# Decode attention on one core: V's fifth tile loaded ahead of K's fifth, DVE's small steps moved behind K's turns, q's copies on ACT, w2 in five pieces

## The chip, the core and the metric

The kernel runs on one core of a Trainium2 chip. The core has five engines that run side by side, each through its own list of instructions in order: TensorE (PE; PEld is its weight load), VectorE (DVE), ScalarE (ACT), GpSimd (POOL) and SyncE (SP), which here issues nearly all DMAs. An instruction waits at the head of its engine's list until the semaphores that it needs are set, and what stands behind it waits too. The metric is the device time of one execution in microseconds (us).

## The reference

One decode step of a transformer block, for 8 sequences with one new token each, all in float32. A conditioning vector c gives six modulations; attention runs over a window of the K and V caches; a feed-forward part with a squared ReLU follows.

```
mod = silu(c) @ w_mod                      # 8 x (6*512): sa, ca, ga, sb, cb, gb
h = layernorm(x) * (1 + ca) + sa           # x: 8 x 1 x 512
q = h @ wq                                 # 32 query heads of 128, 8 key/value heads
k, v = the last 2048 of 8192 cached rows   # 8 sequences x 8 heads x 2048 x 128 each
p = softmax(q k^T / sqrt(128));  o = p v
x = x + ga * (o @ wo)                      # wo: 4096 x 512
h = layernorm(x) * (1 + cb) + sb
x = x + gb * (relu(h @ w1 + b1)^2 @ w2 + b2)   # w1: 512 x 1792, w2: 1792 x 512
```

The K and V windows are 67 MB each, the weights some 31 MB: 165 MB are read for little arithmetic.

## The kernel before, in words

**Tiles and slots.** All loads from HBM go into two sets of buffers in on-chip memory: 2 big slots of 4 MB (`K_SLOTS`) and 5 small ones of 2 MB (`V_SLOTS`). A K tile (`("K", q)`, q = 0 to 15) is half of the sequences of one key/value head and takes a big slot; a V tile (`("V", n)`, n = 0 to 31) is two sequences of one head and takes a small one. w_mod (three pieces) and wo (three tiles of two heads each; the fourth lies in the tail) take small slots, wq (two halves), the tail (last part of wo, first half of w1) and w2 take big ones. With two big slots, K tile q can be loaded only when K tile q - 2 has been used up.

**The order of the loads** is a list, `loads` (L144 to L155), written ahead of time. `pump` (L158) issues its entries in order as long as the next one has a free slot; `done` (L163) frees a slot and pumps. All loads stand in SP's one list, so a load that waits for its slot holds all loads behind it. w2 is issued in four pieces (L136), so that its matmuls can start on the first.

**The main loop** (L494) has 38 steps of a quarter of a head. A step s turns half a K tile: `transposes` (L195) is DVE's 32x32 block transpose of 128x1024 elements, called a turn below, four turns a step; two make one kT tile, of which there are two buffers. `scores` (L349) multiplies it with q on TensorE, four column groups into one PSUM bank `s_ps` for a head. The big slot is free after a tile's eighth turn (L196).

**Softmax of a head** is spread over the two steps behind its last scores. ACT copies the scores out of PSUM (`ss`, L370); DVE takes the maximum of each row (`mx`, L372); TensorE permutes the scores (`p_ps`, L377) and turns the maxima into a row (L380); DVE reduces them over four rows and scales them (`m`, `mrow`, L383, L389); TensorE turns them back into a column; DVE copies it (`nm`, L398); ACT takes the exponential with the row sums `z` (L401) and half of the spread-out copy `pr2` (L409), DVE the other half (L411) and `zs` (L413); DVE transposes it (`pT`, L423), TensorE sums over rows (L428), DVE takes the reciprocal `rz` (L432).

**P V** runs five steps behind (`PV_LAG`). `weighted` (L434) multiplies pT with a V tile in two halves on TensorE; after the second half the V slot is free, and four DVE instructions (L457, L459) add the diagonal blocks into `o_sb`. `gather` (L463) and `project_o` (L478) bring a head's output through wo.

**q.** Two `turn_q` calls (L319) turn the query into `qbd`, the second one at step 1. `window` (L337) spreads one head's q over the four column groups into `qst`: one matmul and eight copies of 32x64 out of PSUM, by turns on ACT and DVE (L345). The first head's stands in front of the first scores, each next head's in front of the scores in the middle of the head before.

**The end.** When the last V tile has been used, the output projection, the second layer norm, w1 and w2 follow, each on the one before; w2's matmuls (L606) go through its 14 row blocks in order.

Of the kernel before, what the change touches and what calls it, by code (L numbers as in the profile page):

```python
# [20 lines left out]
def tile_adaln_cached_attention_mlp(  # L21
# [26 lines left out]
    C = B // 2  # L48
    N = HKV * C
# [39 lines left out]
    def load(key):  # L89
        kind, i = key  # L90
        if kind == "b":
            nc.sync.dma_start(b1_in, b1.rearrange("(g n) -> g n", g=NQ))
            nc.sync.dma_start(b2_in, b2.rearrange("(g n) -> g n", g=NQ))
            return
        held[key] = free[size_of(key)].pop(0)
        t = slots[size_of(key)][held[key]]
        if kind in "KV":


            if kind == "K":  # L100
                v = k_cache[4 * (i % 2) : 4 * (i % 2) + 4, i // 2]
            else:
                v = v_cache[i % C :: C, i // C]
            v = v[:, SK - W :, :].rearrange("u (p j) d -> p u (j d)", p=P // v.shape[0])
            for x in range(2 if key == ("V", N * 2 - 1) else 1):
                cols = slice(x * NJ * DH // 2, (x + 1) * NJ * DH // 2) if key == ("V", N * 2 - 1) else slice(None)
                nc.sync.dma_start(t[:, cols], v[..., cols])
            return

        def rows(o, v):  # L110
            n = v.shape[1] * v.shape[2]
            nc.sync.dma_start(t[:, o : o + n].rearrange("p (a n) -> p a n", n=v.shape[2]), v)

        def wo_rows(j):

            r = 2 * REP * DH
            return wo[j * r : (j + 1) * r, :].rearrange("(h p i) n -> p h (i n)", p=P, i=4)

        w1v = w1.rearrange(r_kc, p=P)
        if kind == "wo":  # L120
            rows(0, wo_rows(i))
        elif kind == "mod":

            nc.sync.dma_start(t, w_mod.rearrange("(p kc) n -> p (kc n)", p=P)[:, i * NJ * DH : (i + 1) * NJ * DH])
        elif kind == "wq":

            nc.sync.dma_start(t, wq.rearrange("(p h a) n -> h p (a n)", p=P, h=2)[i])
        elif kind == "tail":
            for h in range(2):
                rows(h * 4 * D, wo_rows(HKV // 2 - 1)[:, h : h + 1])  # L130
            rows(NJ * DH, w1v[:, 0:2])
        elif kind == "w1":
            rows(0, w1v[:, 2:4])
        else:
            v = w2.rearrange("(p c) n -> p c n", p=P)
            for lo, hi in ((0, 8), (8, 12), (12, 13), (13, 14)):  # L136
                rows(D * lo, v[:, lo:hi])

    def slot(key, n, o=0):
# [2 lines left out]
        return t[:, : t.shape[1] // n * n].rearrange("p (a n) -> p a n", n=n)  # L142

    loads = [*(("mod", k) for k in range(3)), ("wq", 0), ("wq", 1)]  # L144
    loads += [("V", 0), ("K", 0), ("V", 1), ("K", 1), ("V", 2), ("K", 2), ("V", 3), ("K", 3), ("K", 4)]
    late = N // 4
    for v in range(4, N):

        q, odd = divmod(v + 4 if v <= 2 * late - 4 else v + 5, 2)
        if not odd and 4 < q < N // 2:  # L150
            loads.append(("K", q))
        if v % (2 * C) == 2 * C - 4 and v < 6 * C:
            loads.append(("wo", v // (2 * C)))
        loads.append(("V", v))
    loads += [("b", 0), ("tail", 0), ("w1", 0), ("w2", 0)]  # L155
# [25 lines left out]


    qbd = consts.tile([P, HKV, 4, B * REP], F32, name="qbd")
    qst = [consts.tile([P, B, 4, 4, 2, REP], F32, name=f"qst{i}") for i in range(2)]


    KTS = {}
# [142 lines left out]
            )  # L330

    turn_q(0)


    PT_, RZ_, RZP_, OS_, O_, MX_, SS_, X_ = {}, {}, {}, {}, {}, {}, {}, {}

    def window(hk):  # L337

        pq = ps_1.tile([P, 512], F32, name="q_ps")
        nc.tensor.matmul(pq[:, :P], sel, qbd[:, hk].rearrange("p j x -> p (j x)"), start=True, stop=True)  # L340
        pv = pq[:, :P].rearrange("p (j c u t) -> p c u j t", j=4, c=2, u=4)
        for i in range(4):
            b = slice(32 * i, 32 * i + 32)
            for c in range(2):
                (nc.vector.tensor_copy if c else nc.scalar.copy)(  # L345
                    qst[hk % 2][b, 4 * c : 4 * c + 4, :, i, c], pv[b, c]
                )

    def scores(q, j):  # L349

        hk, c = divmod(q, 2)
        if c == 0 and j == 0:
            s_ps[0] = ps_1.tile([P, 512], F32, name="s_ps")
            if hk == 0:
                window(0)
        if c == 1 and j == 0 and hk + 1 < HKV:
            window(hk + 1)
        kT = KTS.pop((q, j)).rearrange("q r (p u) -> q u (r p)", u=4)
        for u in range(4):
            nc.tensor.matmul(  # L360
                s_ps[0][32 * u : 32 * u + 32, :],
                qst[hk % 2][:, 4 * c + u, j].rearrange("p i c t -> p (i c t)"),
                kT[:, u],
                start=(c == 0 and j == 0),
                stop=(c == 1 and j == 3),
            )

    def soft_a(hk):
        ss = work.tile([P, 512], F32, name="ss", tag="a", bufs=1)
        nc.scalar.copy(ss, s_ps[0])  # L370
        mx = work.tile([P, 1], F32, name="mx")
        nc.vector.tensor_reduce(mx, ss, axis=AX.X, op=ALU.max)  # L372
        SS_[hk], MX_[hk] = ss, mx

    def soft_b(hk):
        sp = ps_1.tile([P, 512], F32, name="p_ps")
        nc.tensor.matmul(sp, perm, SS_.pop(hk), start=True, stop=True)  # L377
        SS_[hk] = sp
        pm = ps_m.tile([P, 512], F32, name="m_ps", tag="m_ps")
        nc.tensor.matmul(pm[0:1, :P], MX_.pop(hk), ident, start=True, stop=True)  # L380
        mrow = work.tile([1, 4, 32], F32, name="mrow")
        m1 = work.tile([1, 32], F32, name="m1")
        nc.vector.tensor_reduce(  # L383
            m1.rearrange("p (u r) -> p u r", u=4),
            pm[0:1, :P].rearrange("p (u i r) -> p u r i", u=4, i=4),
            axis=AX.X,
            op=ALU.max,
        )
        nc.vector.tensor_scalar(mrow, m1[:, None, :].to_broadcast([1, 4, 32]), -SCALE, None, op0=ALU.mult)  # L389
        MX_[hk] = mrow  # L390

    def soft_c(hk):
        pm = ps_m.tile([P, 512], F32, name="m_ps", tag="m_ps")
        nc.tensor.matmul(
            pm[:, 0:1], MX_.pop(hk).rearrange("p j r -> p (j r)"), ones[0:1, 0:1], start=True, stop=True
        )
        nm = work.tile([P, 1], F32, name="nm")
        nc.vector.tensor_copy(nm, pm[:, 0:1])  # L398
        pr = work.tile([P, 2, 32, 8], F32, name="pr", tag="a", bufs=1)
        z = work.tile([P, 1], F32, name="z")  # L400
        nc.scalar.activation(  # L401
            pr.rearrange("p e j x -> p (e j x)"), SS_.pop(hk), AF.Exp, bias=nm, scale=SCALE, accum_out=z
        )

        X_[hk] = work.tile([P, 32, 8, 2, 2], F32, name="pr2", bufs=1)
        for c in range(2):
            o, i = X_[hk][:, :, :, :, c], pr.rearrange("p e j x -> p j x e")
            if c:
                nc.scalar.mul(o, i, uq[:, c : c + 1])  # L409
            else:  # L410
                nc.vector.tensor_scalar(o, i, uq[:, c : c + 1], None, op0=ALU.mult)  # L411
        zs = work.tile([P, B], F32, name="zs")
        nc.vector.tensor_scalar(zs, bq, z, None, op0=ALU.mult)  # L413
        RZP_[hk] = zs
# [19 lines left out]
    def weighted(n, h):  # L434
# [6 lines left out]
        for g in range(4):  # L441
# [8 lines left out]
        if h == 0:  # L450
            return
        del O_[n]
        done(("V", n))
# [24 lines left out]
    def project_o(hk):  # L478
# [11 lines left out]
        if hk % 2 and not last:  # L490
            done(("wo", hk // 2))


    for s in range(N + PV_LAG + 1):  # L494
        g, i = divmod(s, C)
# [157 lines left out]
```

## Time and profile before

| | |
|---|---|
| median of 3 runs | 402.33 us (402.02 to 403.03) |
| the profiled execution, its own time | 402.6 us |
| its span, from the first to the last instruction | 400.7 us |
| TensorE busy, DVE busy, ACT busy | 261.9, 246.2, 33.5 us |
| moved by DMA, mean over the span | 165.08 MB, 412 GB/s |
| chain that ended last: DMA, DVE, PE | 63%, 21%, 11% |

How to read it: the page cuts the span into 40 slices, each digit being a busy share in tenths. In the rows of groups and of the timeline stand line, engine, operation, what is written <- what is read, the shape, and in brackets how long the engine idled before it and what ended that. SPq rows are DMA issues; their time is the issue's, not the transfer's. In the chain of waits a DMA row starts at the issue and ends at the landing, so it holds the time that the transfer queued behind others.

### The profile page before, as it was taken

How to read it: one execution, taken by the hardware profiler on the slowest of the kernel's cores; microseconds unless marked ns; L12 is line 12 of the kernel's file. 1: busy time of each engine (PE TensorE's matmuls, PEld its weight loads, DVE VectorE, ACT ScalarE, POOL GpSimd, SP SyncE). 2: the span in 40 equal slices, each digit the busy share in tenths (PEclk: the TensorE clock that was granted, in tenths of full speed). 3: DMA queues.
4: the chain of work that ended last, by engine and by line, in shares of the span. 5: the costliest groups of instructions: out<-in, count | busy, mean ns of one | idle time of the engine just before them, and what ended most of it. 6: DMA issues, size and time to landing. Idle time of an engine off the chain costs nothing.

```text
span 400.7 us, 3775 instructions
## 1 busy us (share of the span) xinstructions
PE 261.9 (65%) x1502; PEld 58.7 (15%) x1502; DVE 246.2 (61%) x436; ACT 33.5 (8%) x81; POOL 0.9 (0%) x7
## 2 busy tenths in 40 slices
PE   0624517656777865887488738974855678867595
PEld 0301101001111110211021102110211011111133
DVE  1630157847867775787578847975738478954331
ACT  1200010002001000100010001000100010030010
POOL 0000000000000000000000000000000000000000
PEclk9978857886989989898999978988997989999799
DMA  8999999995899999999999999999999999999993
GB/s 316 447 432 415 444 429 415 451 422 224 366 406 433 429 442 417 436 425 435 411 448 412 450 409 442 419 440 411 443 415 451 406 443 415 432 430 421 421 426 151
DMA packets 9922, 165.08 MB, mean 412 GB/s; under 512 B 1064, under 2 KB 1328, under 8 KB 1584
## 3 DMA queue, kind: packets, MB, share of 16 engines
q1 hardware_dynamic: 9760, 164.71, 96.6%
q8 instruction: 12, 0.20, 0.2%
q10 hardware_dynamic: 144, 0.13, 0.2%
q14 instruction: 6, 0.05, 0.0%
HBM read 164.77 MB, written 0.07 MB: 411 GB/s over the span
## 4 chain that ended last, share of the span: by engine, by line
DMA 63%; DVE 21%; PE 11%; ACT 2%; issue 1%; SPq 0%; DVEq 0%; ACTq 0%
DMA big<-in_A_k_cache_dram 39%; DVE kT L195 14%; DMA small<-in_A_v_cache_dram 12%; DMA big<-in_A_wq_dram 7%; DMA big<-in_B_w_dram 6%; PE s_ps L360 5%; DVE o_sb L459 3%; PE o_ps L443 3%; DVE qst L345 1%; PE m_ps L309 1%; ACT qst L345 1%; DVE o_sb L457 1%; PE p_ps L377 0%; PE m_ps L606 0%; ACT L401 0%
## 5 line engine op out<-in xcount | busy, mean ns | idle before, releaser
L360 PE MATMUL s_ps<-kT,qst 128*32 128x512 f32 x512 | 127.4, 1074 | 93.5 <-DVE kT L195 77.1
L195 DVE STREAM_TRANSPOSE kT<-big 128x1024 f32<-128x1024 f32 x128 | 151.7, 1219 | 48.4 <-DMA big<-in_A_k_cache_dram 48.3
L443 PE MATMUL o_ps<-small,pT 128*32 128x512 f32 x512 | 74.3, 653 | 7.8 <-DMA small<-in_A_v_cache_dram 7.7
L459 DVE SCALAR_TENSOR_TENSOR o_sb<-o_ps,diag,o_sb 128x128 f32<-128x128 f32 x96 | 33.7, 351 | 3.4
L360 PEld LDWEIGHTS s_ps<-kT,qst 128*32 128x32 f32 x512 | 12.1, 119 | 140.5 <-DVE kT L195 82.3
L443 PEld LDWEIGHTS o_ps<-small,pT 128*32 128x32 f32 x512 | 17.4, 121 | 77.4 <-issue 56.1
L457 DVE TENSOR_SCALAR o_sb<-o_ps,diag 128x128 f32<-128x128 f32 x32 | 10.4, 326 | 19.1 <-PE o_ps L443 19.1
L309 PE MATMUL m_ps<-big,h1T 128*32 128x512 f32 x64 | 10.0, 784 | 12.4 <-DMA big<-in_A_wq_dram 12.4
L327 DVE COPY qbd<-m_ps 32x128 f32<-32x128 f32 x8 | 3.0, 372 | 23.1 <-PE m_ps L324 23.0
L345 ACT COPY qst<-q_ps 32x64 f32<-32x64 f32 x32 | 6.5, 204 | 117.8 <-PE q_ps L340 78.7
L370 ACT COPY ss<-s_ps 128x512 f32<-128x512 f32 x8 | 4.7, 586 | 98.8 <-PE s_ps L360 98.8
L377 PE MATMUL p_ps<-ss,perm 128*128 128x512 f32 x16 | 11.6, 813 | 0.0
L345 DVE COPY qst<-q_ps 32x64 f32<-32x64 f32 x32 | 6.8, 213 | 6.6 <-ACT qst L345 6.5
L401 ACT ACTIVATE pr<-p_ps,nm 128x512 f32<-128x512 f32 x8 | 5.5, 688 | 62.5 <-DVE nm L398 62.5
L467 PE MATMUL m_ps<-o_sb,pick 128*128 128x512 f32 x16 | 9.0, 644 | 2.6 <-DVE o_sb L459 2.6
L423 DVE STREAM_TRANSPOSE pT<-pr 128x1024 f32<-128x1024 f32 x8 | 9.8, 1229 | 0.0
L411 DVE TENSOR_SCALAR pr<-pr,uq 128x512 f32<-128x512 f32 x8 | 4.0, 500 | 8.5 <-ACT pr L401 8.5
L383 DVE TENSOR_REDUCE m<-m_ps 1x32 f32<-1x128 f32 x8 | 2.2, 277 | 11.0 <-PE m_ps L380 11.0
L229 PE MATMUL m_ps<-xsum,sel 128*128 128x1 f32 x2 | 0.6, 363 | 12.7 <-DVE xsum L227 12.7
L372 DVE TENSOR_REDUCE mx<-ss 128x1 f32<-128x512 f32 x8 | 5.2, 654 | 4.4 <-ACT ss L370 4.4
L283 PE MATMUL m_ps<-small,cT 128*32 128x256 f32 (+1 forms) x72 | 7.0, 555 | 0.0
L409 ACT ACTIVATE pr<-pr,uq 128x512 f32<-128x512 f32 x8 | 6.8, 852 | 0.3
(123 smaller groups left out, 110.9 us busy)
## 6 DMA issues: line engine op xcount, KB each, us to landing
small<-in_A_v_cache_dram SPq DMA_DIRECT2D x32, 2048.0 KB, 25.4
big<-in_A_k_cache_dram SPq DMA_DIRECT2D x16, 4096.0 KB, 22.3
big<-in_A_wq_dram SPq DMA_DIRECT2D x2, 4096.0 KB, 31.4
small<-in_w_mod_dram SPq DMA_DIRECT2D x3, 2048.0 KB, 17.3
small<-in_A_wo_dram SPq DMA_DIRECT2D x3, 2048.0 KB, 20.1
big<-in_A_wo_dram SPq DMA_DIRECT2D x2, 1024.0 KB, 21.2
big<-in_B_w_dram SPq DMA_DIRECT2D x1, 2048.0 KB, 24.8
big<-in_B_w_dram SPq DMA_DIRECT2D x1, 1792.0 KB, 25.0
```

The lines of the kernel that those rows point to most:

```text
L195: nc.vector.transpose(KTS[q, j][:, rows], k[:, rows, 32 * j : 32 * j + 32])
L283: nc.tensor.matmul(pms[m // 4][32 * q : 32 * q + 32, m % 4 * P : (m % 4 + n) * P].rearrange("p (m n) -> p m n", n=P), cT[:, kc, :], wv[:, ...
L309: nc.tensor.matmul(pqs[r][32 * g : 32 * g + 32, :], hT[:, kc, :], w[:, 4 * r + g, :], start=(kc == 0), stop=(kc == NQ - 1),)
L345: (nc.vector.tensor_copy if c else nc.scalar.copy)(qst[hk % 2][b, 4 * c : 4 * c + 4, :, i, c], pv[b, c])
L360: nc.tensor.matmul(s_ps[0][32 * u : 32 * u + 32, :], qst[hk % 2][:, 4 * c + u, j].rearrange("p i c t -> p (i c t)"), kT[:, u], start=(c == ...
L377: nc.tensor.matmul(sp, perm, SS_.pop(hk), start=True, stop=True)
L409: nc.scalar.mul(o, i, uq[:, c : c + 1])
L423: nc.vector.transpose(PT_[hk].rearrange("p u j r -> p j u r"), X_.pop(hk).rearrange("p j (u r) e c -> p j u (r e c)", u=4),)
L443: nc.tensor.matmul(o[32 * g : 32 * g + 32].rearrange("p j d -> p (j d)"), PT_[hk][:, c, j : j + 4].rearrange("p i r -> p (i r)"), v[:, j : ...
L457: nc.vector.tensor_scalar(d, o[:, 0, :], diag[:, 0:1], None, op0=ALU.mult)
L459: nc.vector.scalar_tensor_tensor(d, o[:, j, :], diag[:, j : j + 1], d, op0=ALU.mult, op1=ALU.add)
L467: nc.tensor.matmul(pp, pick.rearrange("p t u -> p (t u)"), o.rearrange("p c d -> p (c d)"), start=True, stop=True)
```

## The change

It has four parts.

- **Loads.** V's fifth tile (`("V", 4)`) is put between K's fourth and fifth in the list. wo's first tile, which stood ahead of it, now stands ahead of the sixth V tile; everything behind keeps its place.
- **Small steps.** Softmax is cut into seven pieces (`soft_a` to `soft_g`), and each DVE step stands one turn of K behind the place where it stood, so a turn lies between what it reads and the step. TensorE's transpose of the maxima now stands ahead of the scores of that step instead of behind the permutation. The adding of the diagonal blocks (`parts`) leaves `weighted` and stands behind one more turn.
- **q.** Both `turn_q` calls and the first head's `window` stand ahead of the loop. A head's eight copies become four of 32x128, all on ACT, into a `qst` of a new layout (two blocks with a gap of four between them).
- **w2** is loaded in five pieces instead of four: the middle one, of four row blocks, becomes two of two.

```diff
-            for lo, hi in ((0, 8), (8, 12), (12, 13), (13, 14)):
+            for lo, hi in ((0, 8), (8, 10), (10, 12), (12, 13), (13, 14)):
...
-    loads += [("V", 0), ("K", 0), ("V", 1), ("K", 1), ("V", 2), ("K", 2), ("V", 3), ("K", 3), ("K", 4)]
+    loads += [("V", 0), ("K", 0), ("V", 1), ("K", 1), ("V", 2), ("K", 2), ("V", 3), ("K", 3), ("V", 4), ("K", 4)]
     late = N // 4
-    for v in range(4, N):
+    for v in range(5, N):
...
-        if v % (2 * C) == 2 * C - 4 and v < 6 * C:
+        if v in (5, 3 * C, 5 * C):
             loads.append(("wo", v // (2 * C)))
...
-    qst = [consts.tile([P, B, 4, 4, 2, REP], F32, name=f"qst{i}") for i in range(2)]
+    qst = [consts.tile([P, 2 * (B * P // 2 + REP)], F32, name=f"qst{i}") for i in range(2)]
...
     turn_q(0)
+    turn_q(1)
...
         for i in range(4):
             b = slice(32 * i, 32 * i + 32)
-            for c in range(2):
-                (nc.vector.tensor_copy if c else nc.scalar.copy)(
-                    qst[hk % 2][b, 4 * c : 4 * c + 4, :, i, c], pv[b, c]
-                )
+            nc.scalar.copy(own[b, :, :, i, 0], pq[b, :P].rearrange("p (c m t) -> p c m t", c=2, t=REP))
...
+    def soft_b(hk):
         mx = work.tile([P, 1], F32, name="mx")
-        nc.vector.tensor_reduce(mx, ss, axis=AX.X, op=ALU.max)
-        SS_[hk], MX_[hk] = ss, mx
...
+        nc.vector.tensor_reduce(mx, SS_[hk], axis=AX.X, op=ALU.max)
+        MX_[hk] = ps_m.tile([P, 512], F32, name="m_ps", tag="m_ps")
+        nc.tensor.matmul(MX_[hk][0:1, :P], mx, ident, start=True, stop=True)
...
+    def soft_d(hk):
+        sp = ps_1.tile([P, 512], F32, name="p_ps")
+        nc.tensor.matmul(sp, perm, SS_.pop(hk), start=True, stop=True)
+        SS_[hk] = sp
...
+    window(0)
...
-        if s == 1:
-            turn_q(1)
         if i == 1 and soft:
-            soft_c(g - 1)
+            soft_e(g - 1)
         if s < N:
             transposes(q, 2 * h, 0)
...
             transposes(q, 2 * h, 1)
+        if i == 1 and soft:
+            soft_f(g - 1)
...
-        if i == 1 and soft:
-            soft_d(g - 1)
+        if i == 0 and soft:
+            soft_b(g - 1)
         if s < N:
             transposes(q, 2 * h + 1, 0)
+        if i == 1 and soft:
+            soft_g(g - 1)
+        if i == 0 and soft:
+            soft_c(g - 1)
+        if 1 <= v <= N:
+            parts(v - 1)
         if s < N:
             scores(q, 2 * h)
         if i == 0 and soft:
-            soft_b(g - 1)
+            soft_d(g - 1)
```

How the change moves the loads, on SP, around K's fourth and fifth tile (the rows with `big` are K tiles, `small_91` in the first row is V's fourth tile; the number is the buffer):

```order
 L107 DMA small_91<-in_A_v_cache_dram 128x1x4096
 L107 DMA big_89<-in_A_k_cache_dram 128x1x8192
+L107 DMA small_92<-in_A_v_cache_dram 128x1x4096
 L107 DMA big_88<-in_A_k_cache_dram 128x1x8192
-L112 DMA small_92<-in_A_wo_dram 128x2x2048
-L107 DMA small_93<-in_A_v_cache_dram 128x1x4096
+L112 DMA small_93<-in_A_wo_dram 128x2x2048
 L107 DMA small_94<-in_A_v_cache_dram 128x1x4096
 L107 DMA big_89<-in_A_k_cache_dram 128x1x8192
```

V's fifth tile now goes into the buffer that wo's first tile took, ahead of K's fifth; wo's goes into the buffer of V's first tile, behind it.

On DVE, from the turns of K's third tile on, in which the first head's softmax lies; before:

```order
L195 STREAM_TRANSPOSE kT<-big_88 128x1024
L372 TENSOR_REDUCE mx<-ss 128x1
L195 STREAM_TRANSPOSE kT<-big_88 128x1024 x2
L383 TENSOR_REDUCE m_381<-m_ps 1x32
L389 TENSOR_SCALAR mrow<-m_381 1x128
L195 STREAM_TRANSPOSE kT<-big_88 128x1024
L398 COPY nm<-m_ps 128x1
L411 TENSOR_SCALAR pr_392<-pr,uq 128x512
L413 TENSOR_SCALAR zs<-bq,z 128x8
L195 STREAM_TRANSPOSE kT<-big_88 128x1024 x2
L423 STREAM_TRANSPOSE pT<-pr_392 128x32x4x8
L432 RECIPROCAL rz<-m_ps 128x8
```

and with the change (lines of the changed kernel; its L196 is L195, its L378 L372, its L386 L383, its L406 L398, its L423 L411, its L432 L423):

```order
L196 STREAM_TRANSPOSE kT<-big_88 128x1024 x2
L378 TENSOR_REDUCE mx<-ss 128x1
L196 STREAM_TRANSPOSE kT<-big_88 128x1024
L386 TENSOR_REDUCE m_367<-m_ps 1x32
L392 TENSOR_SCALAR mrow<-m_367 1x128
L196 STREAM_TRANSPOSE kT<-big_88 128x1024
L406 COPY nm<-m_ps 128x1
L196 STREAM_TRANSPOSE kT<-big_88 128x1024 x2
L423 TENSOR_SCALAR pr_385<-pr,uq 128x512
L427 TENSOR_SCALAR zs<-bq,z 128x8
L196 STREAM_TRANSPOSE kT<-big_88 128x1024
L432 STREAM_TRANSPOSE pT<-pr_385 128x32x4x8
```

mx stands behind two turns instead of one, m behind three as before, pr behind two more turns than nm, pT behind one turn more than pr.

More of the change, by code (lines that the diff above doesn't have):

```diff
@@ L339, in window @@
         pq = ps_1.tile([P, 512], F32, name="q_ps")
-        nc.tensor.matmul(pq[:, :P], sel, qbd[:, hk].rearrange("p j x -> p (j x)"), start=True, stop=True)
-        pv = pq[:, :P].rearrange("p (j c u t) -> p c u j t", j=4, c=2, u=4)
+        nc.tensor.matmul(
+            pq[:, :P].rearrange("p (a j t) -> p a j t", j=4, t=REP),
+            sel,
+            qbd[:, hk].rearrange("p j (a t) -> p a j t", t=REP),
+            start=True,
+            stop=True,
+        )
+        own = qst[hk % 2].rearrange("p (c x) -> p c x", c=2)[:, :, : B * P // 2]
+        own = own.rearrange("p c (m i k t) -> p c m i k t", i=4, k=2, t=REP)
         for i in range(4):
             b = slice(32 * i, 32 * i + 32)
-            for c in range(2):
-                (nc.vector.tensor_copy if c else nc.scalar.copy)(
-                    qst[hk % 2][b, 4 * c : 4 * c + 4, :, i, c], pv[b, c]
-                )
+            nc.scalar.copy(own[b, :, :, i, 0], pq[b, :P].rearrange("p (c m t) -> p c m t", c=2, t=REP))
     def scores(q, j):
@@ L353, in scores @@
             s_ps[0] = ps_1.tile([P, 512], F32, name="s_ps")
-            if hk == 0:
-                window(0)
         if c == 1 and j == 0 and hk + 1 < HKV:
@@ L361, in scores @@
                 s_ps[0][32 * u : 32 * u + 32, :],
-                qst[hk % 2][:, 4 * c + u, j].rearrange("p i c t -> p (i c t)"),
+                qst[hk % 2][:, P * (4 * c + u) + 32 * j :][:, :32],
                 kT[:, u],
@@ L368, in soft_a, with soft_c @@
     def soft_a(hk):
-        ss = work.tile([P, 512], F32, name="ss", tag="a", bufs=1)
-        nc.scalar.copy(ss, s_ps[0])
+        SS_[hk] = work.tile([P, 512], F32, name="ss", tag="a", bufs=1)
+        nc.scalar.copy(SS_[hk], s_ps[0])
+    def soft_b(hk):
         mx = work.tile([P, 1], F32, name="mx")
-        nc.vector.tensor_reduce(mx, ss, axis=AX.X, op=ALU.max)
-        SS_[hk], MX_[hk] = ss, mx
[L375 to L380, printed above, removed]
+        nc.vector.tensor_reduce(mx, SS_[hk], axis=AX.X, op=ALU.max)
+        MX_[hk] = ps_m.tile([P, 512], F32, name="m_ps", tag="m_ps")
+        nc.tensor.matmul(MX_[hk][0:1, :P], mx, ident, start=True, stop=True)
+    def soft_c(hk):
+        pm = MX_.pop(hk)
         mrow = work.tile([1, 4, 32], F32, name="mrow")
@@ L390, in soft_b, with soft_e @@
         MX_[hk] = mrow
-    def soft_c(hk):
+    def soft_d(hk):
+        sp = ps_1.tile([P, 512], F32, name="p_ps")
+        nc.tensor.matmul(sp, perm, SS_.pop(hk), start=True, stop=True)
+        SS_[hk] = sp
+    def soft_e(hk):
         pm = ps_m.tile([P, 512], F32, name="m_ps", tag="m_ps")
@@ L405, in soft_c @@
         X_[hk] = work.tile([P, 32, 8, 2, 2], F32, name="pr2", bufs=1)
[L406 to L414, printed above, removed]
+        nc.scalar.mul(X_[hk][:, :, :, :, 1], pr.rearrange("p e j x -> p j x e"), uq[:, 1:2])
+        RZP_[hk] = pr, z
         if hk == HKV - 1:
@@ L418, in soft_c, with soft_f, soft_g @@
             nc.scalar.activation(warm, eps, AF.Sqrt)
-    def soft_d(hk):
+    def soft_f(hk):
+        pr, z = RZP_[hk]
+        nc.vector.tensor_scalar(
+            X_[hk][:, :, :, :, 0], pr.rearrange("p e j x -> p j x e"), uq[:, 0:1], None, op0=ALU.mult
+        )
+        RZP_[hk] = work.tile([P, B], F32, name="zs")
+        nc.vector.tensor_scalar(RZP_[hk], bq, z, None, op0=ALU.mult)
+    def soft_g(hk):
         PT_[hk] = work.tile([P, 4, 32, 2 * REP], F32, name="pT", bufs=1)
@@ L449, in weighted, with parts @@
             )
[L450 to L453, printed above, removed]
+        if h == 1:
+            done(("V", n))
+    def parts(n):
+        hk, c = divmod(n, C)
+        o = O_.pop(n)
         if c == 0:
```

## The prediction

> **What bounds the kernel now.** I read the page's slices first, then windows around the one slice that stands out, then the chain of waits, then the timeline at the stall.
>
> ```profile
> DVE  1630157847867775787578847975738478954331
> DMA  8999999995899999999999999999999999999993
> GB/s 316 447 432 415 444 429 415 451 422 224 366 406 433 429 442 417 436 425 435 411 448 412 450 409 442 419 440 411 443 415 451 406 443 415 432 430 421 421 426 151
> ```
>
> The DMA engines are busy in nearly every slice, DVE never for long; only the tenth and eleventh slices (90 to 110 us) fall, to 224 and 366 GB/s. In windows of 5 us, with the DMA share and GB/s as the last two columns:
>
> ```profile
> 85.00:90.00 5.00, 3.98 (x12) 0.78 (x12) 2.00 (x2) 0.00 (x0) 0.00 (x0) 0.66 1.06 455
> 90.00:95.00 5.00, 2.61 (x13) 0.57 (x11) 2.56 (x7) 2.90 (x4) 0.00 (x0) 0.80 0.99 423
> 95.00:100.00 5.00, 3.39 (x18) 0.90 (x18) 5.00 (x6) 0.00 (x0) 0.00 (x0) 0.51 0.08 33
> 100.00:105.00 5.00, 4.85 (x30) 1.05 (x30) 4.18 (x8) 0.20 (x1) 0.00 (x0) 1.00 0.66 262
> 105.00:110.00 5.00, 2.57 (x20) 0.40 (x16) 4.18 (x7) 0.61 (x3) 0.00 (x0) 1.00 0.99 426
> 96.00:101.50 5.50, 4.27 (x24) 0.75 (x28) 5.50 (x6) 0.00 (x0) 0.00 (x0) 0.65 0.00 0
> ```
>
> From 96.0 to 101.5 us no packet starts at all. Why is in the DMA issues (SPq rows: start, time until the last of them is issued):
>
> ```profile
> 79.31 21.73 SPq L107 DMA_DIRECT2D big<-in_A_k_cache_dram  x2
> 101.10 0.59 SPq L112 DMA_DIRECT2D small<-in_A_wo_dram  x1
> 103.45 9.85 SPq L107 DMA_DIRECT2D small<-in_A_v_cache_dram  x2
> 116.59 0.54 SPq L107 DMA_DIRECT2D big<-in_A_k_cache_dram  x1
> ```
>
> K tile 3 is issued at 79.31, K tile 4 ends its issue at 101.04, so it starts at 100.50 (one issue takes 0.54). It needs the big slot that K tile 2 holds until DVE has turned it, and all later loads stand behind it on the one SP queue, wo's first tile too, whose slot is free. The load queue runs dry, and the traffic restarts 1.0 after K4's issue. How much the kernel pays shows in the chain of waits, where a K row's start plus its length is that tile's landing:
>
> ```profile
> 67.89 14.90 DMA big<-in_A_k_cache_dram
> 116.59 22.22 DMA big<-in_A_k_cache_dram
> 154.21 23.65 DMA big<-in_A_k_cache_dram
> 192.96 23.97 DMA big<-in_A_k_cache_dram
> small<-in_A_v_cache_dram SPq DMA_DIRECT2D x32, 2048.0 KB, 25.4
> big<-in_A_k_cache_dram SPq DMA_DIRECT2D x16, 4096.0 KB, 22.3
> ```
>
> K5 lands at 138.81, K7 at 177.86, K9 at 216.93: 39.05 and 39.07 us for two big and four small tiles, eight times 2.097 MB, so 4.88 us for 2 MB, 430 GB/s. From K2 (82.79) to K5 pass V3, K3, K4, wo, V4, V5 and K5, ten such units, which is 48.8 us at that pace; they take 56.02. **The stall costs 7.2 us by landings.** By bytes it is 6.7: the windows from 90 to 110 us moved 5 x (423 + 33 + 262 + 426) = 5.72 MB, 13.3 us' worth in 20. By busy share it is 6.4: 20 less 5 x (0.99 + 0.08 + 0.66 + 0.99). With no traffic at all it is 5.5.
>
> After it the stream never stops again, and the end hangs on it:
>
> ```profile
> 373.36 3.37 PE L443 MATMUL o_ps<-small,pT 128*32 128x512 f32 x16 [2.41 <-DMA small<-in_A_v_cache_dram]
> 393.27 1.96 PE L606 MATMUL m_ps<-big,rT 128*32 128x128 f32 x64 [0.28 <-DMA big<-in_B_w_dram]
> 395.65 1.69 PE L606 MATMUL m_ps<-big,rT 128*32 128x128 f32 x48 [0.42 <-DMA big<-in_B_w_dram]
> 396.91 0.16 PEld L606 LDWEIGHTS m_ps<-big,rT 128*32 128x32 f32 x8 [0.23 <-DMA big<-in_B_w_dram]
> ```
>
> TensorE waits for the last V tile, then for w2's first, second and last pieces; 3.8 us after that wait the span ends. What the stream gains, the end gains.
>
> **The change part by part.** *V4 ahead of K4.* Its slot, the third of the small ones, last held a piece of w_mod, whose last matmul starts at 21.2:
>
> ```profile
> L283 PE MATMUL m_ps<-small,cT x72: 379/583/1061, 14.6 to 21.2; 128*32 128x256 f32 x48, 128*32 128x512 f32 x24
> ```
>
> So V4 is issued right behind K3, near 80, and its 4.88 us carry the stream from 96.0 to 100.9. For no gap K4 has to be issued by about 99.9, since its first packets come 1.0 after its issue; before, 100.50. V4 leaves its old place, so no bytes are added: the gain is the stall. Of the bounds, 5.5 (only the empty stretch) and 7.2 (all of the excess by landings), I take **6.4**, the mean over the DMA engines by busy share, since the engines drain and restart unevenly and some of that unevenness will remain.
>
> *DVE's small steps.* Whether K4 is early enough is settled in K2's turns (82.91 to 100.50):
>
> ```profile
> 82.91 1.25 DVE L195 STREAM_TRANSPOSE kT<-big 128x1024 f32<-128x1024 f32 x1 [3.62 <-DMA big<-in_A_k_cache_dram]
> 84.08 0.64 DVE L372 TENSOR_REDUCE mx<-ss 128x1 f32<-128x512 f32 x1
> 84.64 2.36 DVE L195 STREAM_TRANSPOSE kT<-big 128x1024 f32<-128x1024 f32 x2
> 90.22 0.28 DVE L383 TENSOR_REDUCE m<-m_ps 1x32 f32<-1x128 f32 x1 [3.22 <-PE m_ps L380]
> 91.84 0.11 DVE L398 COPY nm<-m_ps 128x1 f32<-128x1 f32 x1
> 92.02 1.28 ACT L401 ACT_TABLE_LOAD   x1 [9.99 <-DVE nm L398]
> 94.13 0.49 DVE L411 TENSOR_SCALAR pr<-pr,uq 128x512 f32<-128x512 f32 x1 [2.19 <-ACT pr L401]
> 87.93 1.94 PE L377 MATMUL p_ps<-ss,perm 128*128 128x512 f32 x2
> ```
>
> Eight turns of 1.18 and small steps make up 12.8 of the 17.6 us; DVE idles 3.22 and 2.19 behind PE and ACT. After the change the maximum's transpose stands ahead of the scores on TensorE, so m is ready by about 86.5, when DVE comes to it at 87.1 after three turns and mx. nm still follows p_ps on TensorE: 86.4 + 1.98 (scores) + 1.94 + 0.3 gives 90.6, a wait of 1.8 behind the fourth turn (88.7). The exponential, 1.28 + 0.9 long, is hidden behind two turns (2.36); ACT's multiply and TensorE's sum behind the next. Then 0.5, 0.1, two more turns, 1.2 and 0.1 follow the pair: K2 is free near 97.3. That is an estimate from these rows. What it hides under are K's turns; if none of it came about, K4 would be at 100.5, the second rival.
>
> *What is late next.* wo now waits for V0 (103.45 above), but K4 moves until 100.9 + 9.76 = 110.7, so 7 us remain. V5 was issued at 103.45 + 9.85 - 0.54 = 112.76 and K5 starts to move at 138.81 - 9.76 = 129.05, V5 4.88 before: 11.4 us of reserve. K5 and the later K tiles have 22.3 - 9.8 = 12.5, V tiles 20. With everything 6.4 sooner, at least 5 us are left, even if compute gained nothing. So no second gap.
>
> *q's copies on ACT.* Of the four copies of 32x128 the trace shows only smaller and larger relatives:
>
> ```profile
> L345 ACT COPY qst<-q_ps 32x64 f32<-32x64 f32 x32 | 6.5, 204 | 117.8 <-PE q_ps L340 78.7 <-DVE qst L345 39.1
> L345 DVE COPY qst<-q_ps 32x64 f32<-32x64 f32 x32 | 6.8, 213 | 6.6 <-ACT qst L345 6.5
> L298 ACT COPY ga<-m_ps 128x128 f32<-128x128 f32 x1 | 0.3, 266 | 6.8 <-DVE h_sb L295 6.8
> L370 ACT COPY ss<-s_ps 128x512 f32<-128x512 f32 x8 | 4.7, 586 | 98.8 <-PE s_ps L360 98.8
> DVE kT L195 <- DMA big<-in_A_k_cache_dram: 48.3, 14, 7.4
> ```
>
> Between 4 x 0.204 and 4 x 0.586 a head; by its nearest row (266, same width) 1.1 us. Behind them on ACT stands the next ss copy, a K tile's turns later; ACT idles 98.8 us before that. DVE loses 6.8 us of work and 6.5 of waiting over the run, worth 0 where it waits for K anyway (48.3 us, 14 times). Without that cover it would be worth up to 13.3. The first head's q now comes ahead of K0: it takes room from DVE's idle 7.43 before 53.58, and K0's turns get rid of the steps among them; K2's issue moves up, its transfer does not, since it queues behind V2. Worth 0.
>
> *w2 in five pieces.* Only the matmuls of the last piece stand behind its landing, before and after (8 loads at 396.91): 0, at best -0.15, the 8 less the 0.28 that they need at 1.69/48 each. The last two pieces, 0.52 MB, pass in 396.91 - 395.65 = 1.26 us, 416 GB/s against 430 in the stream: two pieces of 0.5 MB cost at most 0.08 more. The Trainium skill speaks against this edit (DMA: Bandwidth & Descriptors, section Bandwidth): batch to 1 MiB or more for at least 75% of peak. The trace's 416 GB/s for pieces a quarter that size, queued behind others, does not bear it out; by it the sum would end 0.8 later.
>
> **Sum.** The profiled execution is 402.6 us, 1.9 around the span of 400.7, and 0.27 above the median of the runs, 402.33. 402.6 - 6.4 = 396.2; from the median **395.9**.
>
> **The rivals.**
>
> 1. *K4 comes no earlier.* If waits replace those that the new order removes, K4 stays at 100.5, a gap of 0.6 and an uneven drain and restart (7.2 - 5.5 = 1.7) remain: gain 4.9, 397.4. For it: m and nm still hang on TensorE's in-order queue. Against: the two waits of 5.4 us have turns put into them.
> 2. *The gap moves.* Each V slot comes free behind softmax; if each of the five delayed steps costs its full turn, 5 x 1.18 = 5.9, V1 is released at 118.7. V5's reserve of 11.4 less 6.4 is then overdrawn by 0.9; with the first head's waits on top (5.4) the stream stops for 6.3: no change, 402.2. Against: DVE idles there now, and turns fill the wait rather than add to it.
> 3. *Slower: a head's compute becomes the bound.* K's stream is 39.05 a head. The turns of a head take 17.6 with softmax (K2's, above) and 15.1 without (K7's: its landing at 177.86 to K9's issue at 192.96, which takes its slot), 32.7 together. From 6.35 us more a head compute decides. If all five delayed steps (5.9) and four copies at the widest row (2.3) fell on that path, it would be 8.2 more: 1.85 over in each of seven heads, 13.0, less the 6.4: 408.9. For it: DVE and TensorE are in order, so one late step holds all behind it. Against: it needs every step unhidden, and both engines idle for over a third of the span:
>
> ```profile
> PE 261.9 (65%) x1502; PEld 58.7 (15%) x1502; DVE 246.2 (61%) x436; ACT 33.5 (8%) x81; POOL 0.9 (0%) x7
> ```
>
> 4. *The change does not reorder what counts*: V4's slot taken, 402.3. Against: the last reader of that slot is long done (21.2, above).
> 5. *Small pieces cost* 3.25 instead of 2.44 for w2's middle megabyte (75% of 430 GB/s): 396.7. The Trainium skill (DMA: Bandwidth & Descriptors, section Bandwidth) has the rule that would make them so slow.
>
> **How the numbers follow.** Forecast 60% (395.9, own range 395.1, the whole 7.2, to 396.8, the empty stretch alone); first rival 20% (to 399.2, if K4 were some 1.8 later than before); second 8%; third 4%; fourth 2%; fifth 3%; 3% for more gain than 7.2. About 0.3%, 1.2 us, is what a measurement tells from no change. Faster 0.86, same 0.10, slower 0.04. For 8 in 10 the range runs from 394.9 to 399.2.
>
> **What would show it.** Right: no window at 96 to 102 below 400 GB/s, K4's landing 9.7 after V4's, K5 landing near 132, DVE's idle before m and pr gone, TensorE still waiting for w2's last piece, near 390.5. Wrong: an empty stretch elsewhere (a V or K row of SPq issued less than 5 us before its transfer), DVE no longer waiting for K tiles, or the last wait no longer a DMA's.

## The result

The changed kernel takes 396.4 us, the median of 4 runs (396.19 to 398.41), against 402.36 before (402.02 to 403.03); the ratio is 0.9861, 95% interval 0.9827 to 0.9895. The forecast was 395.9 in a range of 394.9 to 399.2. The profiled execution takes 396.19 us, its span 394.4.

The slices of the page, after:

```profile
DVE  1620354857978756965687568747829287954332
DMA  8999999999999999999999999999999999999993
GB/s 326 432 435 429 450 432 405 447 424 420 434 420 435 429 440 414 451 405 450 409 443 414 442 415 437 424 430 419 449 412 442 415 447 417 427 425 422 428 416 130
```

The dip of the tenth and eleventh slices is gone. In windows of 5 us around it (share and GB/s are the last two columns):

```profile
90.00:95.00 5.00, 3.75 (x18) 0.52 (x18) 4.98 (x7) 2.91 (x4) 0.00 (x0) 1.00 0.99 426
95.00:100.00 5.00, 4.65 (x30) 0.90 (x26) 3.64 (x5) 0.17 (x1) 0.00 (x0) 1.00 0.96 410
100.00:105.00 5.00, 3.92 (x24) 0.76 (x28) 4.89 (x9) 0.85 (x4) 0.00 (x0) 1.00 1.07 462
```

The issues on SP, where the row at 78.37 is V4, the big one at 96.50 K4, the row at 99.44 wo's first tile:

```profile
77.79 0.54 SPq L107 DMA_DIRECT2D big<-in_A_k_cache_dram  x1
78.37 0.60 SPq L107 DMA_DIRECT2D small<-in_A_v_cache_dram  x1
96.50 0.54 SPq L107 DMA_DIRECT2D big<-in_A_k_cache_dram  x1
99.44 0.40 SPq L112 DMA_DIRECT2D small<-in_A_wo_dram  x1
106.83 0.54 SPq L107 DMA_DIRECT2D small<-in_A_v_cache_dram  x1
```

V4 goes out right behind K3, and K4 is issued while V4's data are on the way. The chain of waits gives the landings, as a row's start plus its length:

```profile
109.82 22.11 DMA big<-in_A_k_cache_dram
143.94 27.09 DMA big<-in_A_k_cache_dram
183.05 27.05 DMA big<-in_A_k_cache_dram
222.11 27.00 DMA big<-in_A_k_cache_dram
306.31 27.22 DMA big<-in_A_k_cache_dram
```

K5 lands at 131.93 instead of 138.81, 6.9 us sooner; K7 at 171.03 and K9 at 210.10, 6.8 sooner each (K11 is the row between them and the last). K15, the last row, lands at 333.53; before, DVE's wait for it ended at 338.91 (timeline):

```profile
338.91 1.25 DVE L195 STREAM_TRANSPOSE kT<-big 128x1024 f32<-128x1024 f32 x1 [1.36 <-DMA big<-in_A_k_cache_dram]
```

That is 5.4 sooner, so the landings of the last K tiles show less of the gain than K5's; the last section comes back to it. The turns of K2 on DVE, with the first head's softmax:

```profile
83.26 2.37 DVE L196 STREAM_TRANSPOSE kT<-big 128x1024 f32<-128x1024 f32 x2 [5.50 <-DMA big<-in_A_k_cache_dram]
85.56 0.64 DVE L378 TENSOR_REDUCE mx<-ss 128x1 f32<-128x512 f32 x1
87.38 0.28 DVE L386 TENSOR_REDUCE m<-m_ps 1x32 f32<-1x128 f32 x1
90.02 0.16 DVE L406 COPY nm<-m_ps 128x1 f32<-128x1 f32 x1 [0.95 <-PE m_ps L402]
92.38 0.48 DVE L423 TENSOR_SCALAR pr<-pr,uq 128x512 f32<-128x512 f32 x1
95.28 1.19 DVE L196 STREAM_TRANSPOSE kT<-big 128x1024 f32<-128x1024 f32 x1
```

m (3.22 us of idle time before) and pr (2.19) no longer wait; nm waits 0.95. m and nm stand behind as many turns as before, so m's wait went because TensorE now transposes the maxima ahead of the scores, not because DVE's step moved. K2 is free at 96.5, 13.2 us after DVE began on it instead of 17.6. DVE now waits longer for K tiles, 78.1 us instead of 48.3 (view of waits: us, times, longest):

```profile
DVE kT L196 <- DMA big<-in_A_k_cache_dram: 78.1, 16, 7.8
```

ACT's copies of q take 257 ns each (group: busy us, mean ns, idle before):

```profile
L353 ACT COPY qst<-q_ps 32x128 f32<-32x128 f32 x32 | 8.2, 257 | 79.5 <-PE q_ps L342 79.2
```

At the end TensorE runs through w2's first thirteen row blocks without a wait and waits, briefly, only for the last piece:

```profile
387.51 3.04 PE L626 MATMUL m_ps<-big,rT 128*32 128x128 f32 x104
390.71 0.43 PE L626 MATMUL m_ps<-big,rT 128*32 128x128 f32 x8 [0.15 <-DMA big<-in_B_w_dram]
```

The wait is 0.15 us, so the work of the last layers is nearly as late there as the stream.

### The profile page after: what moved, and what is told of

The parts are those of the page before. It is cut to its first block, busy times and chain, and to the rows that moved or that the text cites. A ratio compares the mean times of both kernels' runs of the same rounds, so it can differ in the third digit from the quotient of the medians.

```text
span 394.4 us, 3760 instructions
## 1 busy us (share of the span) xinstructions
PE 261.5 (66%) x1502; PEld 59.8 (15%) x1502; DVE 238.5 (60%) x404; ACT 35.2 (9%) x81; POOL 0.9 (0%) x7
## 4 chain that ended last, share of the span: by engine, by line
DMA 73%; DVE 19%; PE 3%; issue 3%; SPq 1%; ACT 0%; DVEq 0%; ACTq 0%
DMA big<-in_A_k_cache_dram 44%; DVE kT L196 14%; DMA small<-in_A_v_cache_dram 9%; DMA big<-in_A_wq_dram 9%; DMA big<-in_B_w_dram 5%; DMA big<-in_A_wo_dram 5%; DVE o_sb L471 4%; PE m_ps L310 2%; PE s_ps L364 1%; DVE o_sb L469 1%; PE o_ps L452 0%; SPq L124 0%; DVE mx L378 0%; ACT ss L374 0%; SPq L127 0%
## 5 line engine op out<-in xcount | busy, mean ns | idle before, releaser
L196 DVE STREAM_TRANSPOSE kT<-big 128x1024 f32<-128x1024 f32 x128 | 151.5, 1220 | 78.2 <-DMA big<-in_A_k_cache_dram 78.1
L364 PE MATMUL s_ps<-kT,qst 128*32 128x512 f32 x512 | 129.7, 1075 | 33.1 <-DVE kT L196 32.9
L452 PE MATMUL o_ps<-small,pT 128*32 128x512 f32 x512 | 70.2, 629 | 4.9 <-DMA small<-in_A_v_cache_dram 4.9
L380 PE MATMUL m_ps<-ident,mx 128*1 128x128 f32 x16 | 4.3, 366 | 48.1 <-DVE mx L378 48.1
L452 PEld LDWEIGHTS o_ps<-small,pT 128*32 128x32 f32 x512 | 16.4, 121 | 83.6 <-issue 66.4
L364 PEld LDWEIGHTS s_ps<-kT,qst 128*32 128x32 f32 x512 | 14.1, 115 | 68.3 <-DVE kT L196 53.5
L310 PE MATMUL m_ps<-big,h1T 128*32 128x512 f32 x64 | 12.3, 940 | 12.3 <-DMA big<-in_A_wq_dram 12.3
L479 PE MATMUL m_ps<-o_sb,pick 128*128 128x512 f32 x16 | 10.0, 707 | 12.3 <-DVE o_sb L471 12.3
L353 ACT COPY qst<-q_ps 32x128 f32<-32x128 f32 x32 | 8.2, 257 | 79.5 <-PE q_ps L342 79.2
L432 DVE STREAM_TRANSPOSE pT<-pr 128x1024 f32<-128x1024 f32 x8 | 9.7, 1207 | 0.2 <-ACT pr L414 0.2
L483 DVE STREAM_TRANSPOSE tr<-m_ps 128x512 f32<-128x512 f32 x8 | 5.7, 716 | 3.8 <-PE m_ps L479 3.4
L378 DVE TENSOR_REDUCE mx<-ss 128x1 f32<-128x512 f32 x8 | 5.2, 650 | 2.8 <-ACT ss L374 2.8
## 6 DMA issues: line engine op xcount, KB each, us to landing
small<-in_A_v_cache_dram SPq DMA_DIRECT2D x32, 2048.0 KB, 27.7
```

What stands on the lines that cost most here:

```text
L196: nc.vector.transpose(KTS[q, j][:, rows], k[:, rows, 32 * j : 32 * j + 32])
L310: nc.tensor.matmul(pqs[r][32 * g : 32 * g + 32, :], hT[:, kc, :], w[:, 4 * r + g, :], start=(kc == 0), stop=(kc == NQ - 1),)
L353: nc.scalar.copy(own[b, :, :, i, 0], pq[b, :P].rearrange("p (c m t) -> p c m t", c=2, t=REP))
L364: nc.tensor.matmul(s_ps[0][32 * u : 32 * u + 32, :], qst[hk % 2][:, P * (4 * c + u) + 32 * j :][:, :32], kT[:, u], start=(c == 0 and j == ...
L432: nc.vector.transpose(PT_[hk].rearrange("p u j r -> p j u r"), X_.pop(hk).rearrange("p j (u r) e c -> p j u (r e c)", u=4),)
L452: nc.tensor.matmul(o[32 * g : 32 * g + 32].rearrange("p j d -> p (j d)"), PT_[hk][:, c, j : j + 4].rearrange("p i r -> p (i r)"), v[:, j : ...
```

## The experiments

The theory: the stall is a dry load queue, the kernel before and after it is bound by the stream of loads, and the change pays because the stream no longer stops. The first rival: the small steps on DVE are the gain. The second: compute is close behind the stream and would soon be the bound. All ratios and gains are against the kernel before on the same chip: 402.63 us for the order of the loads, everything but it, q's copies and w2, 402.69 for the doubled turns. The changed kernel's 396.4 comes from the result above, where the kernel before took 402.36, so a few tenths between it and a run of an experiment are not to be read from the times alone.

### The order of the loads alone

```diff
-    loads += [..., ("K", 3), ("K", 4)]
+    loads += [..., ("K", 3), ("V", 4), ("K", 4)]
-    for v in range(4, N):
+    for v in range(5, N):
-        if v % (2 * C) == 2 * C - 4 and v < 6 * C:
+        if v in (5, 3 * C, 5 * C):
```

> The kernel before with the new order of the loads only (V4 ahead of K4, wo's first tile ahead of V5); DVE's steps, q's copies and w2 as before. Theory (the stall is a dry load queue; V4 fills it, and the small steps only bring K4 forward): K2 is still free at 100.5, V4's transfer lasts to about 100.9 on the mean engine, so 0.5 to 1 us stay empty and the engines drain and restart unevenly: a gain of about 4.9, 397.4 us; the slices from 90 to 110 us above 380 GB/s. If the small steps are not needed at all: 396.4, as with the whole change. Rival (the small steps are what helps, the order of loads only moves a wait): 402.4.

Measured: 398.11 us (397.4 to 398.34), 0.9875 of before, 0.9847 to 0.9903: a gain of 4.5. K4 is issued at 100.84 (timeline):

```profile
100.84 0.54 SPq L107 DMA_DIRECT2D big<-in_A_k_cache_dram  x1
```

and the window from 100 to 105 still moves only 256 GB/s (last column):

```profile
100.00:105.00 5.00, 5.00 (x33) 0.98 (x29) 4.14 (x7) 0.20 (x1) 0.00 (x0) 0.87 0.65 256
```

The order of the loads by itself gives about three quarters of the gain, 0.4 us less than expected. K4 comes too late to join up with V4: of the page's slices from 90 to 110 us the first moves 425 GB/s, but the second 334, where more than 380 was expected.

### Everything but the order of the loads

```diff
-    loads += [..., ("K", 3), ("V", 4), ("K", 4)]
+    loads += [..., ("K", 3), ("K", 4)]
     (and the two lines behind it as before; the rest as changed)
```

> The changed kernel with the old order of the loads: small steps, q's copies and w2 as changed. Theory: K4 is issued at 96.5 as in the profile after instead of 100.5, but K3's traffic ends at 96.0 and K4's begins 1.0 after its issue, so 1.5 us stay empty instead of 5.5, with an uneven drain and restart: a gain of about 4, 398.4 us. Rival (only the order of the loads counts): 402.4. Rival (the steps alone do it all): 396.4.

Measured: 399.38 us (399.02 to 399.49), 0.9907, 0.9886 to 0.9929: a gain of 3.25, between the two rivals and 1 us less than expected. K4's issue starts at 78.32 + 19.69 - 0.53 = 97.48, 1 us later than in the changed kernel (timeline; the row holds K3's and K4's issue):

```profile
78.32 19.69 SPq L107 DMA_DIRECT2D big<-in_A_k_cache_dram  x2
```

The window from 95 to 100 moves 131 GB/s instead of 33:

```profile
95.00:100.00 5.00, 4.86 (x32) 0.61 (x24) 4.11 (x6) 0.00 (x0) 0.00 (x0) 1.00 0.39 131
```

and K5 lands at 110.33 + 25.43 = 135.76 by the chain of waits:

```profile
110.33 25.43 DMA big<-in_A_k_cache_dram
```

So the steps work through the same gap: they bring K4 forward, and the order of the loads covers what is left. The two gains, 4.5 and 3.25, add up to more than the 6.0 of both, as they must if there is one gap, which can be closed only once. The run has q's and w2's edits too; K2's turns hold no copy of q in either kernel.

### K2's turns made longer

Some turns of K2 are done twice with the same data, so that K4 is issued later; the order of the loads and all else in the program stay as changed. Three turns, and then all eight:

```diff
-        nc.vector.transpose(KTS[q, j][:, rows], k[:, rows, 32 * j : 32 * j + 32])
+        for _ in range(2 if (q, e) == (2, 1) and j > 0 else 1):      # the second: if q == 2
+            nc.vector.transpose(KTS[q, j][:, rows], k[:, rows, 32 * j : 32 * j + 32])
```

> The changed kernel with three of K2's eight turns done twice (the same data again), some 3.6 us of DVE work in front of K4's issue. Theory (K4 has only to be issued before V4's transfer ends, by about 99.9; it is issued at 96.5): K4 comes at about 100, no stretch without traffic, 396.4 to 397. Rival (every us by which K4 is late counts): 400.

Measured: 397.0 us (396.43 to 397.59), 0.9867, 0.9843 to 0.9892. K4 is issued 3.2 us later than in the changed kernel, at 99.72 (timeline):

```profile
99.72 0.54 SPq L107 DMA_DIRECT2D big<-in_A_k_cache_dram  x1
```

The window from 100 to 105 falls to 331 GB/s, and half a microsecond in it to 98:

```profile
100.00:105.00 5.00, 5.00 (x30) 1.06 (x26) 4.89 (x8) 1.02 (x4) 0.00 (x0) 1.00 0.86 331
100.50:101.00 0.50, 0.50 (x8) 0.15 (x4) 0.50 (x2) 0.00 (x0) 0.00 (x0) 1.00 0.23 98
```

and K5 lands at 111.56 + 21.32 = 132.88 by the chain of waits, 0.95 later than in the changed kernel:

```profile
111.56 21.32 DMA big<-in_A_k_cache_dram
```

The time is inside the expected 396.4 to 397, at its upper end. No stretch is quite without traffic, as expected, but the 98 GB/s say that an issue at 99.72 is already too late, though the theory allowed 99.9. The profiled execution takes 0.64 us more than the changed kernel's (396.83 against 396.19) and the median 0.6; set against the kernel before on each chip the gains are 5.7 and 6.0, so these runs do not tell the difference from none. The trace does.

> The changed kernel with all of K2's eight turns done twice, some 9.4 us in front of K4's issue. Theory: K4 comes at about 105.5, the stream stops from 100.9 to 106.5, and what it loses is not made up later: 5.6 to 7 us more than the changed kernel, 402 to 403.5. Rival (the queue's reserve makes it up): 396.4.

Measured: 402.84 us (402.46 to 403.18), 1.0007, 0.9991 to 1.0023, so the whole gain is gone with K4 issued at 105.94 (timeline):

```profile
105.94 0.53 SPq L107 DMA_DIRECT2D big<-in_A_k_cache_dram  x1
```

The two windows around it move 56 and 210 GB/s:

```profile
100.00:105.00 5.00, 3.58 (x18) 0.66 (x18) 4.93 (x6) 0.00 (x0) 0.00 (x0) 0.66 0.13 56
105.00:110.00 5.00, 4.03 (x22) 0.91 (x26) 4.93 (x7) 0.70 (x3) 0.00 (x0) 1.00 0.59 210
```

K5 lands at 139.25 (117.79 + 21.46, chain of waits) instead of 131.93:

```profile
117.79 21.46 DMA big<-in_A_k_cache_dram
```

V5 and K5 are issued some 8 us later here than in the changed kernel as well, at 114.81 and 117.79, but that stops nothing: K5 lands 21.46 us behind its issue, more than twice the 9.76 that its own data take, and the windows from 110 to 115 and from 115 to 120 move 419 and 415 GB/s. This pins the cause down: with the same order of loads, the same small steps and the same q, the time hangs on whether K4's issue comes in time. By the medians the first 3.2 us of lateness cost 0.6 (small, as said above), the next 6.2 cost 5.8. What the stream loses there, it hardly makes up in the 250 us behind (how much of it, the last section tells).

### How far compute is behind the stream

Turns are done twice in every K tile from the fourth on, four of eight and then six of eight:

```diff
-        nc.vector.transpose(KTS[q, j][:, rows], k[:, rows, 32 * j : 32 * j + 32])
+        for _ in range(2 if e == 1 and q > 2 else 1):                # the second: if j > 0 and q > 2
+            nc.vector.transpose(KTS[q, j][:, rows], k[:, rows, 32 * j : 32 * j + 32])
```

> The changed kernel with four of eight turns done twice in every K tile from the fourth on, 9.4 us more a head. Theory from the profile after (a head's turns take 16.2 with softmax and 12.0 without, 28.2, against 39.05 of transfers): 37.6 a head is still below the transfers: 396.4 to 397. By the prediction's third rival, which took 32.7 a head and a limit of 6.35: 3.05 a head over for six and a half heads, 20 more, less what the queue holds in reserve: 404 to 416.

Measured: 398.29 us (398.26 to 398.31), 0.9898, 0.9871 to 0.9925, 1.9 us over the changed kernel. That misses both expectations: it is 1.3 over the theory's 396.4 to 397, and far below the 404 to 416 of the other. The limit of 6.35 us a head, from which the prediction's third rival would decide, falls: 9.4 us a head do not stop the stream, whose last landing comes only 0.4 later (391.07 against 390.66). What is lost is lost at the end, which the theory had left out, where TensorE no longer waits for w2 at all (timeline: all 112 matmuls in one stretch, no wait in brackets):

```profile
389.86 3.27 PE L627 MATMUL m_ps<-big,rT 128*32 128x128 f32 x112
```

DVE's waits for K tiles (view of waits: us, times, longest) are down from 78.1 to 27.6, not to nothing:

```profile
DVE kT L197 <- DMA big<-in_A_k_cache_dram: 27.6, 9, 5.5
```

> The same with six of eight turns done twice, 14.1 us more a head. Theory: 42.3 a head against 39.05, 3.3 over in six and a half heads, 21, less some 11 that a K tile waits in the queue after its issue: 10 more, 404 to 418, with DVE no longer waiting for K tiles at the end. By the limit of 6.35: 7.75 a head over, 50 more, 440.

Measured: 424.08 us (423.79 to 424.37), 1.0539, 1.0509 to 1.0569; both expectations missed. Two K tiles, one head, are 184.25 to 227.61, 43.4 us, so compute is the bound:

```profile
184.25 0.53 SPq L107 DMA_DIRECT2D big<-in_A_k_cache_dram  x1
204.62 0.54 SPq L107 DMA_DIRECT2D big<-in_A_k_cache_dram  x1
227.61 0.53 SPq L107 DMA_DIRECT2D big<-in_A_k_cache_dram  x1
```

4.3 us over the stream's 39.05 in six and a half heads is 28, and 27.7 is what was measured. The expectation was 17.7 short, for two reasons: it took 11 us off for the time that K tiles wait in the queue, and it had 42.3 us a head instead of 43.4, 1.1 us less in each of six and a half heads. A reserve in the queue keeps the stream going, but once compute sets the pace, its whole length counts. So the limit lies between 9.4 and 14.1 us a head.

### q's copies on DVE, and w2 in four pieces

```diff
-            nc.scalar.copy(own[b, :, :, i, 0], pq[b, :P]...)
+            nc.vector.tensor_copy(own[b, :, :, i, 0], pq[b, :P]...)
```

> The changed kernel with the four copies of each head's q on DVE instead of ACT (32 copies of some 0.25 us). Theory: DVE waits for K tiles for 78 us in the profile after, so 1 us a head is hidden: 396.4, within 0.3. Rival (DVE's time is what the copies were costing): 8 us of DVE work come back, 404.

Measured: 396.28 us (396.18 to 396.4), 0.9832, 0.9811 to 0.9853, the same as with the copies on ACT. 9.1 us of copies go onto DVE (group of the copies: busy us, mean ns, idle before)

```profile
L353 DVE COPY qst<-q_ps 32x128 f32<-32x128 f32 x32 | 9.1, 285 | 0.4
```

and its waiting for K tiles shrinks from 78.1 to 67.4 (view of waits):

```profile
DVE kT L196 <- DMA big<-in_A_k_cache_dram: 67.4, 16, 7.8
```

```diff
-            for lo, hi in ((0, 8), (8, 10), (10, 12), (12, 13), (13, 14)):
+            for lo, hi in ((0, 8), (8, 12), (12, 13), (13, 14)):
```

> The changed kernel with w2 in four pieces again. Theory: only the last piece's eight matmuls stand behind the last landing either way: 396.4, within 0.2. Rival (pieces under 1 MiB run at three quarters of the stream, which the Trainium skill's page DMA: Bandwidth & Descriptors, section Bandwidth, would have): 0.8 faster than the changed kernel, 395.6.

Measured: 396.69 us (396.21 to 398.0), 0.9847, 0.982 to 0.9874: no difference that these runs can tell; their spread would hide the rival's 0.8. The landings, from the traces' semaphore updates, decide it: the megabyte in one piece lands 2.44 us after the piece before it, in two pieces 2.46, where the rival has 3.25 for two. The Trainium skill's rule on batching (DMA: Bandwidth & Descriptors, section Bandwidth) promises at least 75% of peak from 1 MiB on; the rival's 75% for smaller pieces was an estimate from it. These two pieces, queued behind others in a full stream, do not bear it out.

## Why the prediction was right

**The bound.** The stream of loads sets the end, before and after: w2's last piece is still the last wait, and K2's eight doubled turns cost all of the gain, though of the issues that moved with them only K4's came too late for the stream.

**The stall's price.** The step took 6.4 from bounds of 5.5 and 7.2, as the mean over the DMA engines, and on that mean it holds. A load's landing is told by 16 semaphore updates; by their mean, K2 to K5 takes 55.43 us before and 48.97 after, 6.46 less. The reason given for staying below 7.2, that some unevenness would remain, does not hold: by the last updates K2 to K5 now takes 131.93 - 83.14 = 48.79, all of the 48.8 that ten units need at the stream's pace. The profiled executions differ by 402.6 - 396.19 = 6.4, to the tenth what the sum said (396.2), and that is partly luck. Two effects that the sum did not have nearly cancel: K2 itself lands 0.28 sooner on the mean, and at the end the last update lags 0.54 more behind the mean than before (last section). That leaves 6.2 at the last landing, and 0.2 more comes behind it. In the runs' medians the gain is 6.0.

**K4 in time.** K2's turns were worked out to end near 97.3; they end at 96.5. The steps of that working hold: the maximum's transpose ahead of the scores takes m's wait away, the exponential lies behind two turns, nm waits, 0.95 us instead of the estimated 1.8. One step was mis-sized, though it did not decide here: the deadline for K4's issue, 99.9. It counts 1.0 us from an issue to its first data, from a window that ended at 101.5. In the kernel before, no data start to move until 101.8:

```profile
96.00:101.80 5.80, 4.57 (x24) 0.82 (x28) 5.80 (x7) 0.00 (x0) 0.00 (x0) 0.67 0.00 0
101.80:102.00 0.20, 0.20 (x4) 0.00 (x0) 0.20 (x1) 0.00 (x0) 0.00 (x0) 1.00 4.01 1311
```

That is 1.3 us behind the issue at 100.50, and the empty stretch is 5.8 us long rather than 5.5. (A window counts a packet where it starts, so 0.2 us can show more than the engines can move.) It is the same with K2's eight turns twice, where K4 is issued at 105.94:

```profile
102.50:107.20 4.70, 2.54 (x16) 0.51 (x20) 4.67 (x6) 0.00 (x0) 0.00 (x0) 0.84 0.00 0
107.20:107.40 0.20, 0.20 (x4) 0.00 (x0) 0.20 (x1) 0.00 (x0) 0.00 (x0) 1.00 5.87 1638
```

With V4's data all but gone by 100.5 (three turns twice, above), K4 has to be issued by about 99.2, an estimate from these rows. The changed kernel keeps that by 2.7 us, the run with three turns twice misses it by 0.5.

**What is late next: nothing.** V5 is issued at 106.83 and K5 at 109.82, 5.9 and 6.8 us sooner than before, not merely as late as before, as the reserves had assumed. So the second rival, the gap that moves, did not come about.

**Edits costed at nothing.** q's copies: 257 ns each against the 266 of the nearest row, and the time is the same with them on either engine; four copies against eight, and `turn_q` ahead of the loop, were not run by themselves. w2's pieces: 0, by the landings.

**The rivals.** The first (K4 no earlier) is what the order of the loads alone does: 398.1 measured, 397.4 worked out. The fourth falls with V4's issue at 78.37, the fifth with w2's landings. The third was wrong in its limit: it took 32.7 us of compute a head from the turns of the kernel before, and those held waits for TensorE and ACT, 5.4 us in K2's alone, which the change for the most part took away. After the change a head's turns take 28.2. On DVE (timeline):

```profile
112.47 2.37 DVE L196 STREAM_TRANSPOSE kT<-big 128x1024 f32<-128x1024 f32 x2 [2.68 <-DMA big<-in_A_k_cache_dram]
131.95 3.50 DVE L196 STREAM_TRANSPOSE kT<-big 128x1024 f32<-128x1024 f32 x3 [2.27 <-DMA big<-in_A_k_cache_dram]
```

and on SP the issues into the slots that they free:

```profile
128.68 0.54 SPq L107 DMA_DIRECT2D big<-in_A_k_cache_dram  x1
143.94 0.53 SPq L107 DMA_DIRECT2D big<-in_A_k_cache_dram  x1
```

K4's turns run from 112.47 to 128.7, K5's from 131.95 to 143.9 (each ends with the issue): 16.2 and 12.0. A bound read from busy engines with their waits is too tight.

## What to carry to other kernels

In a kernel that lives on one in-order stream of loads, look for the place where the stream stands still, and ask which load at the head of the queue waits for a slot and which one behind it does not; that one can go ahead at no cost, as long as the load whose place it takes is not late in turn. An issue is free if it comes early enough before the transfers in front of it end (here by the 1.3 us from the issue to the first data), and later than that it costs nearly its full time, since this full stream made nothing up. Work off that stream (here 1 us of copies a head, on either engine) changes nothing until it outgrows the stream or makes the end behind the last load later (9.4 us of turns a head cost 1.9 there), and the limit has to be read from work without the waits in it.

## What was not expected of the hardware

Each of these loads tells its landing by 16 semaphore updates, and the time between the first and the last of them is how far its slowest part is behind its fastest. Taken from the traces' updates, in us: this spread at K3, at K4 and at w2's last piece; the mean of the 16 updates at K5 and at w2's last piece; and that piece's last update.

```
kernel                            spread K3     K4     last     mean K5     last     landed
before                                 2.06   0.65     3.38      137.17   394.83     396.87
loads alone                            1.98   0.78     3.21      132.75   390.36     392.32
all but the loads                      2.29   0.45     3.28      134.29   391.95     393.87
three of K2's turns twice              1.83   0.97     3.39      131.69   389.34     391.22
eight of K2's turns twice              2.26   0.47     3.35      137.78   395.46     397.40
changed                                2.12   2.14     4.18      130.43   388.08     390.66
changed, w2 in four                    1.91   1.92     4.42      130.69   388.31     391.04
changed, q on DVE                      1.77   1.79     4.15      130.58   388.24     390.75
changed, four turns twice              1.83   1.84     4.21      130.84   388.48     391.07
changed, six turns twice               2.01   2.03     1.51      130.80   411.40     412.64
```

On the mean, nothing is made up and nothing is lost: from K5 to the last piece the stream takes 257.61 to 257.68 us in nine kernels, and more only in the one in the last row, whose stream stops again and again. The 6.74 us between the kernel before and the changed one at K5 are 6.75 at the end.

The kernel waits for the last update, though, and there something comes back. Where the stream stopped in front of K4, even for a moment, the spread falls to 0.5 to 1.0 and ends at 3.2 to 3.4, the last update 1.9 to 2.0 behind the mean; where it did not, the spread stays near 2 and ends at 4.2 to 4.4, the last update 2.5 to 2.7 behind. So the changed kernel's lead of 6.9 over the kernel before at K5 is 6.2 at the last landing, and its leads over the other four that stopped shrink by 0.4 to 0.7 as well. K15, 5.4 sooner by its last update, is 6.75 sooner by the mean.

That the stop itself causes the smaller spread 290 us later is not shown: before, the spread is back at 2.03 with V5, and the kernels part only near the end (in the changed one it is 2.22 at K12, 3.25 at V19, 3.71 at K15, while before it is 2.08 at K15). What makes one part fall behind, step by step in the course of a run, was not tried and stays open.
